# Where the sums of the second product live: accumulators in SBUF, or copies added by DMAs into DRAM

## The chip, the cores and the metric

One core of a Trainium2 chip runs the kernel. The metric is the time of one execution in device microseconds; less is better. The matrix products run on TensorE (PE in the profile, its weight loads PEld), the elementwise work on VectorE (DVE) and ScalarE (ACT), some on GpSimd (POOL); SyncE (SP) issues most transfers. Each engine has one queue and takes its instructions in order. Products accumulate in PSUM, in banks of 512 f32 per partition.

## The reference

```python
def reference(q, k, v, shift_k, ssm_k, ssm_D, w1, w2):   # S=2048, D=576, Dff=4608
    x  = q
    xn = layernorm(x)
    # H3: a short causal convolution of k, times v, then a long one over S by FFT
    k_shift = sum(k_pad[:, t:t + S] * shift_k[:, ks - 1 - t] for t in range(4))
    kv = k_shift * v
    y  = irfft(rfft(pad(kv)) * rfft(pad(ssm_k)))[:S] + kv * ssm_D
    a  = xn * y
    # feed-forward
    b  = relu(xn @ w1) @ w2
    return x + a + b
```

The sum `x + a + b` has a row for each of the 2048 positions and 576 columns. All of it is f32; the kernel splits each f32 operand of a product into a high and a low part (names `hi`, `lo`, `hh`, `ll`) and multiplies three of the four pairs.

## The kernel before, in words

**Two jobs share the core.** The feed-forward part (FFN) is a fixed sequence of "visits"; the long convolution is a generator, `conv`, whose steps are issued in between.

**The FFN.** The 4608 hidden columns are cut into `NPAIR` = 18 weight pairs of 256 columns, the 2048 rows into `NB` = 4 blocks b of 512. A half of the run treats two blocks (`HB` = 2): for each pair n it visits both blocks s, so there are 72 visits. In a visit, `quad` (L538) makes the first product in four stages, with seven products by sums of operands in place of eight, and two PSUM banks `psb` and `psa`. ScalarE copies one product to `m5`; VectorE adds it to the banks (the pair's sums, L574 and L577); `relu` (L528) writes `hh` on ScalarE (L531) and `ll` on VectorE (L532). The second product is cut into `unit`s (L589): one 128-row tile t (i in a block), one half h of the columns (`NH` = 288), 6 or 12 matmuls into a bank `pso`, of which there are three. `phase` puts eight units of a block into a list, and `fill` takes some after each stage of a quad.

**The sums.** Behind its matmuls a unit adds its bank on VectorE into an accumulator in SBUF, which was loaded with x: for block 0 with the layernorm's factor `rstd` (L610, `scalar_tensor_tensor`), else plainly (L614). A unit's bank is free for the next but two when that add is done. The accumulators of the first half go to DRAM (`fin`) when complete, and the last stage of the convolution adds them to its rows and stores these; those of the second half get the convolution's rows added (L935) and are stored by the last units, the very last row tile by SP and ScalarE's queue (L618).

**The convolution.** A Fourier transform by matmuls with constant matrices, in stages: z (nothing of it yet), loading `kt`; k (transform of `ssm_k`: `stack` splits a tile `ks` on ScalarE L649 and VectorE L650, `first` multiplies and copies the bank on ScalarE, L657); x (the short convolution on VectorE, rows `c` and `e`, L742 to L751, then `xs` split and multiplied in the same way); m (the products of the spectra and the inverse step); o (the last transform; rows `y`, gated with the normalized x at L927 by VectorE, added up at L935). Constants come by POOL's DMAs, into three buffers.

**Who sets the order.** `tick(cost)` is called after each stage of a quad and every six matmuls of a unit. It counts the FFN's work and lets `conv` take one step when it has fallen behind its share; a step's price is one of `W_FK`, `W_FX`, `W_FM`, `W_FO`. Inside a step, `here()` holds elementwise instructions back in their queue until the places of `done["acc"]` and `done["act"]`, the last sum on VectorE and the last marked activation on ScalarE, so that they stand right behind these. Before, `done["acc"]` is set by the units' adds alone.

**The weights.** SP loads them (`r`), ScalarE rounds them to the high part (L453, L511), POOL subtracts for the low part (L424) and makes the sums of weights (L478).

Of the kernel before, what the change touches and what calls it, by code (L numbers as in the profile page):

```python
# [49 lines left out]
SHARE = 0.96  # L50
# [3 lines left out]
W_FK, W_FX, W_FM, W_FO = 1.73, 3.5, 1.94, 2.2  # L54
# [6 lines left out]
SUMS = {"b11": 0, "t1": 1, "t2": 2, "t3": 3, "t4": 4}  # L61
# [44 lines left out]
def h3_ffn_kernel(ctx: ExitStack, tc, x, k, v, shift_k, ssm_k, ssm_D, w1, w2, fwd, inv, mid, out):  # L106
# [23 lines left out]
    fin = dram.tile([HT // 2, P, 2, D], F32, name="fin")  # L130
# [23 lines left out]
    def load_x(t, tag, bufs, **queues):  # L154
        pair = xp.tile([P, 2, D], F32, tag=tag, name=f"acc{t}", bufs=bufs)
        move(pair, x, slice(t, t + 2), **queues)
        return pair

    def load_acc(t, **queues):
        pairs[t] = load_x(t, f"acc{t // BT % HB}", BT // 2, **queues)  # L160
        acc[t], acc[t + 1] = pairs[t][:, 0, :], pairs[t][:, 1, :]
# [120 lines left out]
    def first_xT(srcs):  # L282
# [5 lines left out]
        neg = zp.tile([P, BT], F32, tag="neg", name="neg")  # L288
        behind = None
        for t in range(BT):  # L290
            if t % 2 == 0:
                pair = row_tiles(t)
            xn = pair[:, t % 2, :]
            if t % 2 == 0:
                with tc.issue_after(behind.ins) if behind else nullcontext():
                    stats(t, srcs[t])
                    behind = centred(xn, srcs[t], t)
            else:
                nc.scalar.activation(xn, srcs[t], AF.Copy, scale=-1.0 / D,
                                     accum_out=neg[:, t:t + 1])  # L300
                done["act"] = nc.scalar.activation(xn, srcs[t], AF.Identity,
                                                   bias=neg[:, t:t + 1])
# [11 lines left out]
        with tc.issue_after(done["dve"].ins):  # L314
            for t in range(1, BT, 2):
                stats(t, srcs[t])
            inv_std(0, BT)

    def second_xT(srcs):
# [7 lines left out]
        xn = []  # L327
        for t in range(BT, HT):
            if t % 2 == 0:
                pair = row_tiles(t)  # L330
            xn.append(pair[:, t % 2, :])
            normalized(xn[-1], srcs[t], t)
# [229 lines left out]
    def quad(n, s, m):  # L562
# [11 lines left out]
        nc.vector.tensor_tensor(pa[:, other], pb[:, first], m5, OP.add)  # L574
        yield
        run_seq(pb[:, first], product(n, s, "s3", "t3"))
        nc.vector.tensor_tensor(pb[:, other], pb[:, first], m5, OP.add)  # L577
# [9 lines left out]
    work = []  # L587

    def unit(ns, s, b, i, h, last):  # L589
# [15 lines left out]
        for i, (a, m) in enumerate(seq):  # L605
            nc.tensor.matmul(ps[:, :NH], a, m, start=i == 0, stop=i == len(seq) - 1)  # L606
            if i % 6 == 5:
                tick(6 * NH)
        if b == 0:
            done["acc"] = nc.vector.scalar_tensor_tensor(  # L610
                acc[t][:, dc], ps[:, :NH], rstd[:, t:t + 1], acc[t][:, dc],
                op0=OP.mult, op1=OP.add)
        else:
            done["acc"] = nc.vector.tensor_tensor(acc[t][:, dc], ps[:, :NH], acc[t][:, dc],  # L614
                                                  OP.add)
        if final and t == T - 1:
            for u, queue in ((0, nc.sync), (1, nc.scalar)):
                queue.dma_start(out[u, :, t, dc], acc[t][halves(u)[0], dc])  # L618
        elif last and h:
            if t < HT:  # L620
                if t % 2:
                    nc.sync.dma_start(fin[t // 2], pairs[t - 1])
            elif t == T - 2:
                move(acc[t], out, t, store=True)
            elif t % 2:
                move(pairs[t - 1], out, slice(t - 1, t + 1), store=True)
# [38 lines left out]

    def conv():
# [3 lines left out]

        with tc.tile_pool(name="fk", bufs=2) as fp:
# [18 lines left out]
            def prepare(t, h):  # L690
                stk = fp.tile([P, NH], F32R, tag="stk", name=f"ks{t}_{h}", bufs=3)
# [22 lines left out]

# [440 lines left out]
```

## Time and profile before

| | |
|---|---|
| time, median of 3 runs | 1132.33 us (1128.83 to 1133.09) |
| the profiled execution, its time | 1130.09 us |
| the profiled execution, its span | 1128.1 us, mean granted clock 0.98 |
| instructions in the span | 21092 |
| bytes moved by DMA | 166.75 MB, mean 148 GB/s |
| span, stage z / k / gap / x | 0 to 204 / 204 to 309 / 309 to 343 / 343 to 547 us |
| span, gap / m / gap / o / tail | to 571 / to 953 / to 974 / to 1110 / to 1128.1 us |

A row of a view by stretches gives, per engine, the busy time and in parentheses the number of instructions, then the granted clock as a share of full speed, the mean busy share of 16 DMA engines (it can go over 1 where packets overlap) and GB/s. A row of groups gives line, engine, operation, out<-in by the program's names, shape and type, count, then busy time in us, mean ns of one, and the engine's idle time just before them with what ended it. A row of the waits gives who waited for whom: us in total, times, longest. A row of the timeline gives start, length, and in brackets the idle time ahead. The stages' bounds were taken from the first and last instruction of each.

### The profile page before, as it was taken

The page shows a single profiled execution, that of the slowest core. Times are in us where ns is not written, and L with a number is a line of the kernel's source. Part 1 is how long each engine was busy: PE and PEld are TensorE (multiplying, and loading weights), DVE is VectorE, ACT ScalarE, POOL GpSimd, SP SyncE. Part 2 cuts the span into 40 slices and gives each one's busy share as a digit, 9 for nine tenths or more (in the row PEclk, how much of TensorE's full clock was granted, in tenths as well). Part 3 has the DMA queues.
Part 4 walks back from the last instruction along what each step waited for, and adds up shares of the span by engine and source line. Part 5 has one row for each costly group of instructions (what it writes and reads, how often), then busy time and mean ns, then how long its engine had stood idle before and what let it go on. Part 6 is the DMA issues. An engine that isn't in the chain of part 4 may idle for free.

```text
span 1128.1 us, 21092 instructions
## 1 busy us (share of the span) xinstructions
PE 1067.1 (95%) x7761; PEld 1025.5 (91%) x7761; DVE 803.6 (71%) x1309; ACT 668.3 (59%) x1454; POOL 489.6 (43%) x492
## 2 busy tenths in 40 slices
PE   8979998999988798898999999999999999999998
PEld 5779998999988788898998999999999999999897
DVE  5578733677759999888466667676576665589985
ACT  4434422798824444443368878888887887465451
POOL 3243444455435444564433344433343443545541
PEclk9998998999998999998999999999999999999999
DMA  6035598355574554453894434442334432666654
GB/s 173 25 96 189 214 147 133 114 161 165 167 200 143 159 149 136 140 166 106 300 321 129 128 108 119 121 135 87 111 113 133 119 116 93 168 176 175 206 167 105
DMA packets 139154, 166.75 MB, mean 148 GB/s; under 512 B 47566, under 2 KB 99536, under 8 KB 138541
## 3 DMA queue, kind: packets, MB, share of 16 engines
q1 hardware_dynamic: 126156, 151.24, 46.7%
q0 software_dynamic: 12576, 13.44, 5.2%
q8 instruction: 61, 1.00, 0.4%
q10 hardware_dynamic: 320, 0.74, 0.3%
q14 instruction: 41, 0.33, 0.1%
HBM read 122.12 MB, written 43.25 MB: 147 GB/s over the span
## 4 chain that ended last, share of the span: by engine, by line
PE 67%; DVE 17%; DMA 5%; SPq 4%; issue 3%; ACT 3%; POOL 1%; POOLq 0%; DVEq 0%; ACTq 0%
PE pso L606 28%; PE psb L525 18%; PE psa L525 8%; PE psf L824 6%; DVE e L745 3%; SPq L679 3%; PE psh L525 2%; DVE c L746 2%; PE psf L656 2%; DMA r<-in_w 1%; DVE xs L650 1%; DVE ll L532 1%; DVE acc L614 1%; DVE acc L610 1%; DVE c L751 1%
## 5 line engine op out<-in xcount | busy, mean ns | idle before, releaser
L606 PE MATMUL pso<-w,hh 128*128 128x288 f32 x2304 | 469.9, 298 | 11.0 <-DVE acc L610 6.9
L606 PEld LDWEIGHTS pso<-w,hh 128*128 128x128 f32 x2304 | 371.6, 190 | 20.9 <-DVE acc L610 7.8
L424 POOL TENSOR_TENSOR g<-r,g 128x512 fp32r<-128x512 f32 (+2 forms) x178 | 207.4, 1174 | 379.2 <-ACT g L453 297.4
L606 PE MATMUL pso<-w,ll 128*128 128x288 f32 x1152 | 320.8, 297 | 3.9 <-DVE ll L532 3.9
L525 PE MATMUL psb<-t,g 128*128 128x256 f32 x1632 | 248.2, 287 | 26.2 <-DVE psa L574 14.1
L525 PEld LDWEIGHTS psb<-t,g 128*128 128x128 f32 x1632 | 220.3, 191 | 33.7 <-DVE psa L574 16.7
L606 PEld LDWEIGHTS pso<-w,ll 128*128 128x128 f32 x1152 | 211.3, 190 | 6.5 <-DVE ll L532 4.8
L424 POOL TENSOR_TENSOR w<-r,w 128x576 fp32r<-128x576 f32 x72 | 114.6, 1593 | 73.1 <-ACT w L511 72.9
L478 POOL TENSOR_TENSOR r<-r 128x256 f32<-128x256 f32 x136 | 115.6, 868 | 62.2 <-DMA r<-in_w 59.8
L614 DVE TENSOR_TENSOR acc<-pso,acc 128x288 f32<-128x288 f32 x224 | 96.7, 450 | 57.7 <-PE pso L606 56.9
L525 PE MATMUL psa<-b,g 128*128 128x256 f32 x816 | 122.1, 286 | 0.0
L531 ACT ACTIVATE hh<-psa 128x512 fp32r<-128x512 f32 x68 | 40.7, 598 | 127.2 <-PE psa L525 126.8
L525 PEld LDWEIGHTS psa<-b,g 128*128 128x128 f32 x816 | 109.8, 193 | 0.2
L453 ACT ACTIVATE g<-r 128x512 fp32r<-128x512 f32 (+2 forms) x178 | 91.2, 535 | 29.3 <-POOL r L478 12.1
L532 DVE SCALAR_TENSOR_TENSOR ll<-psa,hh 128x512 fp32r<-128x512 f32 x68 | 46.7, 686 | 39.7 <-ACT hh L531 39.5
L531 ACT ACTIVATE hh<-psb 128x512 fp32r<-128x512 f32 x68 | 40.7, 598 | 49.3 <-PE psb L525 46.5
L532 DVE SCALAR_TENSOR_TENSOR ll<-psb,hh 128x512 fp32r<-128x512 f32 x68 | 46.6, 686 | 29.1 <-ACT hh L531 28.7
L650 DVE TENSOR_TENSOR ks<-kt,ks 64x288 fp32r<-64x288 f32 x64 | 54.4, 849 | 17.3 <-ACT ks L649 15.7
L525 PE MATMUL psb<-b,g 128*128 128x256 f32 x408 | 62.1, 286 | 0.0
L860 DVE TENSOR_TENSOR k<-psf,k 128x288 f32<-128x288 f32 x64 | 28.8, 454 | 46.0 <-ACT sw L859 37.9
L525 PEld LDWEIGHTS psb<-b,g 128*128 128x128 f32 x408 | 55.1, 193 | 0.0
L610 DVE SCALAR_TENSOR_TENSOR acc<-pso,rstd,acc 128x288 f32<-128x288 f32 x80 | 39.4, 511 | 19.7 <-PE pso L606 19.1
(138 smaller groups left out, 1778.7 us busy)
## 6 DMA issues: line engine op xcount, KB each, us to landing
r<-in_w SPq DMA_DIRECT2D x72, 288.0 KB, 4.0
r<-in_w SPq DMA_DIRECT2D x35, 512.0 KB, 4.1
zk<-zk SPq DMA_DIRECT2D x32, 288.0 KB, 2.7
zx<-zx SPq DMA_DIRECT2D x32, 288.0 KB, 3.5
ztk<-zk SPq DMA_DIRECT2D x32, 288.0 KB, 3.1
ztx<-zx SPq DMA_DIRECT2D x32, 288.0 KB, 2.9
zy<-vo SPq DMA_DIRECT2D x32, 288.0 KB, 3.4
zo<-zy SPq DMA_DIRECT2D x32, 288.0 KB, 3.6
```

Source lines behind the costliest of these rows:

```text
L424: return nc.gpsimd.tensor_tensor(dst, src, hi, OP.subtract)
L453: nc.scalar.activation(hi, src, AF.Copy)
L478: nc.gpsimd.tensor_tensor(dst, a, b, op)
L525: nc.tensor.matmul(ps, a, m, start=start and i == 0, stop=i == len(seq) - 1, skip_group_check=not start)
L531: done["act"] = nc.scalar.activation(hh, ps, AF.Relu)
L532: lows.append(nc.vector.scalar_tensor_tensor(ll, ps, 0.0, hh, op0=OP.max, op1=OP.subtract))
L606: nc.tensor.matmul(ps[:, :NH], a, m, start=i == 0, stop=i == len(seq) - 1)
L610: done["acc"] = nc.vector.scalar_tensor_tensor(acc[t][:, dc], ps[:, :NH], rstd[:, t:t + 1], acc[t][:, dc], op0=OP.mult, op1=OP.add)
L614: done["acc"] = nc.vector.tensor_tensor(acc[t][:, dc], ps[:, :NH], acc[t][:, dc], OP.add)
L650: nc.vector.tensor_tensor(dst[other], src[own], dst[own], OP.subtract)
L679: nc.sync.dma_start(kt[halves(h)[0], d:d + KD, :], src)
L824: nc.tensor.matmul(ps[:, :NH], a, m[:, cols], start=n == 0, stop=n == 2)
```

## The change

- A DRAM buffer `total`, [4, 128, 4, 576], takes the place of `fin` and of all accumulators in SBUF. Eight transfers from DRAM to DRAM put x into it at the start.
- A unit copies its bank into one half of a tile `g` in SBUF: ScalarE (L630, L635) in stages z, x and o, VectorE (L632, L637) in k and m. For block 0 the copy multiplies with `rstd`. Each second unit has POOL issue a transfer that adds the tile (288 KB) into `total`. `g` has four buffers.
- The second half's last units load their part of `total` back (`load_total`, into tiles of the same ring), add the bank on VectorE and store the halves; both blocks now go row tile by row tile. The convolution's rows y for the second half are added into `total` by POOL's transfers.
- `done["acc"]` is set by the pair's sums as well, so the convolution's VectorE work can stand right behind them.
- `tick` takes steps once per unit (behind its first six matmuls) and up to two at a stage of a quad; the steps' prices change.
- In o, the gate's normalization goes to ScalarE (an activation with `rstd` and `shift`), VectorE multiplies. Some buffers become more (`stk`, `k`, `zt`); the first rows of x are normalized in place.

The diff, its core:

```diff
-SHARE = 0.96
+SHARE = 0.965
-W_FK, W_FX, W_FM, W_FO = 1.73, 3.5, 1.94, 2.2
+W_FK, W_FX, W_FM, W_FO = 1.875, 3.98, 2.02, 2.03
+BY_ACT = "zxo"
+G_BUFS = 4
...
-    fin = dram.tile([HT // 2, P, 2, D], F32, name="fin")
+    total = dram.tile([NB, P, BT, D], F32, name="total")
...
+    def load_total(t, h):
+        b, i = divmod(t, BT)
+        pair = xp.tile([P, 2, NH], F32, tag="g", name=f"last{t}_{h}", bufs=G_BUFS)
+        nc.sync.dma_start(pair, total[b, :, i:i + 2, h * NH:(h + 1) * NH])
+        for n in range(2):
+            acc[t + n, h] = pair[:, n]
...
     def quad(n, s, m):
-        nc.vector.tensor_tensor(pa[:, other], pb[:, first], m5, OP.add)
+        done["acc"] = nc.vector.tensor_tensor(pa[:, other], pb[:, first], m5, OP.add)
...
-        nc.vector.tensor_tensor(pb[:, other], pb[:, first], m5, OP.add)
+        done["acc"] = nc.vector.tensor_tensor(pb[:, other], pb[:, first], m5, OP.add)
...
     def unit(ns, s, b, i, h, last):
-        for i, (a, m) in enumerate(seq):
-            nc.tensor.matmul(ps[:, :NH], a, m, start=i == 0, stop=i == len(seq) - 1)
-            if i % 6 == 5:
-                tick(6 * NH)
+        for c, (a, m) in enumerate(seq):
+            nc.tensor.matmul(ps[:, :NH], a, m, start=c == 0, stop=c == len(seq) - 1)
+            if c % 6 == 5:
+                tick(6 * NH, c == 5)
+        if final:
+            if h == 0 and i % 2 == 0:
+                for m in range(2):
+                    load_total(t, m)
+            to = acc[t, h]
+            done["acc"] = nc.vector.tensor_tensor(to, ps[:, :NH], to, OP.add)
+            for u, queue in ((0, nc.sync), (1, nc.scalar if t == T - 1 else nc.sync)):
+                queue.dma_start(out[u, :, t, dc], to[halves(u)[0]])
+            return
+        if i % 2 == 0:
+            g = xp.tile([P, 2, NH], F32, tag="g", name=f"sum{ns[0]}_{t}_{h}", bufs=G_BUFS)
+            parts_[0] = g
+        to, src = parts_[0][:, i % 2], ps[:, :NH]
+        act = stage[0] in BY_ACT
         if b == 0:
-            done["acc"] = nc.vector.scalar_tensor_tensor(
-                acc[t][:, dc], ps[:, :NH], rstd[:, t:t + 1], acc[t][:, dc],
-                op0=OP.mult, op1=OP.add)
+            if act:
+                done["act"] = nc.scalar.activation(to, src, AF.Copy, scale=rstd[:, t:t + 1])
+            else:
+                done["acc"] = nc.vector.tensor_scalar(to, src, rstd[:, t:t + 1], None,
+                                                      op0=OP.mult)
+        elif act:
+            done["act"] = nc.scalar.activation(to, src, AF.Copy)
         else:
-            done["acc"] = nc.vector.tensor_tensor(acc[t][:, dc], ps[:, :NH], acc[t][:, dc],
-                                                  OP.add)
...
+            done["acc"] = nc.vector.tensor_copy(to, src)
+        if i % 2:
+            nc.gpsimd.dma_start(total[b, :, i - 1:i + 1, dc], parts_[0], accum_op=OP.add)
...
     def phase(ns, s, b, last):
-        if last and b == NB - 1:
+        if last and b >= HB:
...
              def gate(i):
-                        nc.vector.scalar_tensor_tensor(ys[i], rest[i][1], mv[:, t, 0:1], ys[i],
-                                                       op0=OP.subtract, op1=OP.mult)
+                        q = rest[i][1]
+                        nc.scalar.activation(q, q, AF.Identity, scale=rstd[:, t:t + 1],
+                                             bias=shift[:, t:t + 1])
+                        nc.vector.tensor_tensor(ys[i], ys[i], q, OP.mult)
...
              def add(i):
+                        nc.gpsimd.dma_start(total[t // BT, :, t % BT, :], ys[i],
+                                            accum_op=OP.add)
...
-    def tick(cost):
+    def tick(cost, steps=1):
+        was = clock["ffn"]
+        clock["ffn"] += cost
+        if clock["done"] or was < clock["until"]:
             return
         clock["conv"] += rate[0] * cost
+        for _ in range(steps):
+            if clock["conv"] < 0:
+                return
...
          load_w2(1, h)
+    for b in range(NB):
+        for u in range(U):
+            nc.sync.dma_start(total[b, halves(u)[0]], x[u, :, b * BT:(b + 1) * BT, :])
...
-                tick(W_STAGE[st])
+                tick(W_STAGE[st], 2)
```

What this moves is seen best in the queues. A row is a line, an operation, out<-in with serial numbers, and a shape. First VectorE in stage x, in the visit of pair 12 and its first block, from the pair's second sum (L577, in the changed kernel L581) on. Before:

```order
L577 TENSOR_TENSOR psb12_1_4566<-psb12_1_4566,m5_12_1_4580 128x256
L745 TENSOR_TENSOR e6_3_4606<-k3_4046,sk_3443 128x576
L746 TENSOR_TENSOR c6_4525<-c6_4525,e6_3_4606 128x576
L610 SCALAR_TENSOR_TENSOR acc0_95<-pso11_1_1_4833,rstd_84,acc0_95 128x288
L532 SCALAR_TENSOR_TENSOR ll12_1_0_4679<-psa12_1_4567,hh12_1_0_4678 128x512
L751 TENSOR_TENSOR c6_4525<-c6_4525,v6_4466 128x576
L745 TENSOR_TENSOR e7_1_4715<-k6_4463,sk_3443 128x576
L610 SCALAR_TENSOR_TENSOR acc2_98<-pso11_2_1_4876,rstd_84,acc2_98 128x288
L746 TENSOR_TENSOR c7_4699<-c7_4699,e7_1_4715 128x576
L650 TENSOR_TENSOR xs6_0_4659<-c6_4525,xs6_0_4659 64x576
```

Now, on VectorE at the same place:

```order
L581 TENSOR_TENSOR psb12_1_4670<-psb12_1_4670,m5_12_1_4684 128x256
L760 TENSOR_TENSOR c7_4834<-k7_4746,sk_3514 128x576
L763 TENSOR_TENSOR e7_1_4851<-k6_4564,sk_3514 128x576
L536 SCALAR_TENSOR_TENSOR ll12_1_0_4782<-psa12_1_4671,hh12_1_0_4781 128x512
L764 TENSOR_TENSOR c7_4834<-c7_4834,e7_1_4851 128x576
L663 TENSOR_TENSOR xs6_0_4788<-c6_4642,xs6_0_4788 64x576
L663 TENSOR_TENSOR xs6_1_4802<-c6_4642,xs6_1_4802 64x576
L763 TENSOR_TENSOR e7_2_4891<-k5_4406,sk_3514 128x576
L536 SCALAR_TENSOR_TENSOR ll12_1_1_4822<-psb12_1_4670,hh12_1_1_4821 128x512
L764 TENSOR_TENSOR c7_4834<-c7_4834,e7_2_4891 128x576
L578 TENSOR_TENSOR psa13_1_4863<-psb13_1_4862,m5_13_1_4876 128x256
```

The units' adds (`acc<-pso`) are gone from the queue, and a visit holds ten rows of the convolution between its four rows of the pair. Second, SP at the end of the program. Before, its last rows:

```order
L898 DMA zo31_13886<-zy_87 128x576
L910 DMA ft7_13741<-fin_88 128x576
L150 DMA out_0<-acc8_6989 64x1152 x2
L150 DMA out_0<-acc10_6992 64x1152 x2
L150 DMA out_0<-acc12_6740 64x1152 x2
```

Now, SP's last rows (`last` are the tiles loaded back from `total`; x2 and x4 count transfers in a row):

```order
L621 DMA out_0<-last10_1_14403 64x288 x2
L167 DMA last12_1_14465<-total_88 128x2x288
L621 DMA out_0<-last10_1_14403 64x288 x2
L621 DMA out_0<-last10_0_14401 64x288 x2
L621 DMA out_0<-last10_1_14403 64x288 x2
L621 DMA out_0<-last12_0_14463 64x288 x2
L621 DMA out_0<-last12_1_14465 64x288 x2
L621 DMA out_0<-last12_0_14463 64x288 x2
L621 DMA out_0<-last12_1_14465 64x288 x2
L167 DMA last14_0_14507<-total_88 128x2x288
L167 DMA last14_1_14509<-total_88 128x2x288
L621 DMA out_0<-last14_0_14507 64x288 x2
```

The last tiles' loads from `total` stand behind the stores of the tiles before them. Third, SP near the start. Before:

```order
L150 DMA acc4_226<-in_x 64x1152 x2
L150 DMA acc6_229<-in_x 64x1152 x2
L435 DMA r1_1_232<-in_w1 128x4x256
L437 DMA r1_1_232<-in_w1 64x256 x2
L444 DMA r2_1_0_239<-in_w2 128x2x288
```

Now, on SP:

```order
L151 DMA acc4_228<-in_x 64x1152 x2
L151 DMA acc6_231<-in_x 64x1152 x2
L1068 DMA total_88<-in_x 64x2304 x8
L439 DMA r1_1_234<-in_w1 128x4x256
L441 DMA r1_1_234<-in_w1 64x256 x2
```

The eight transfers into `total` now stand ahead of the second pair's w1 (`r1_1`). ScalarE splits that w1 a little later in its queue, now ahead of the second block's first copies (`b1_1`):

```order
L182 ACTIVATE q4_314<-q4_314 128x4
L630 ACTIVATE sum0_2_1_461<-pso0_2_1_454,rstd_84 128x288
L630 ACTIVATE sum0_2_1_461<-pso0_3_1_463,rstd_84 128x288
L457 ACTIVATE g1_0_472<-r1_1_234 128x512
L226 ACTIVATE b1_1_296<-psf_325 128x512
```

In the kernel before, those copies (`b1_1`, L218) follow the row of `q4` at once, and the split of the second pair stands behind them.

More of the change, by code (lines that the diff above doesn't have):

```diff
@@ L326, in second_xT @@
             inv_std(BT, BT)
[L327 to L332, printed above, removed]
+        xn = [srcs[t] for t in range(BT, HT)]
+        for i, row in enumerate(xn):
+            normalized(row, row, BT + i)
         for c in range(5):
@@ L664, in here @@
             yield
+    stage = ["z"]
+    shift = const.tile([P, T], F32, name="shift")
     def conv():
+        stage[0] = "k"
         with tc.tile_pool(name="fk", bufs=2) as fp:
@@ L932, in add @@
                     t = order[i]
-                    to, more = (ys[i], rest[i][2]) if t < HT else (acc[t], acc[t])
-                    with here():
-                        nc.vector.scalar_tensor_tensor(to, ys[i], rstd[:, t:t + 1], more,
-                                                       op0=OP.mult, op1=OP.add)
                     if t < HT:
-                        move(to, out, t, store=True, queues=(nc.gpsimd, nc.gpsimd))
-                    else:
+                        with here():
+                            nc.vector.tensor_tensor(ys[i], ys[i], rest[i][2], OP.add)
+                        move(ys[i], out, t, store=True, queues=(nc.gpsimd, nc.gpsimd))
+                    else:
+                        nc.gpsimd.dma_start(total[t // BT, :, t % BT, :], ys[i],
+                                            accum_op=OP.add)
                         added.add(t)
-            for n in range(2):
+            for n in range(3):
                 load_z(n)
@@ L1120, in h3_ffn_kernel @@
             phase([n], s, b, True)
-        if half == 1 and m == 0:
-            base = HT + (1 - second) * BT
-            for t in range(base, base + BT, 2):
-                load_acc(t)
     while work:
```

78 lines of the change are left out of this document (33 added, 45 removed).

## The prediction

> **What bounds the kernel now.** I read the busy times first, then the span cut at the stages of the convolution, then the chain, the waits and one engine's groups in the stage that loses most.
>
> ```profile
> PE 1067.1 (95%) x7761; PEld 1025.5 (91%) x7761; DVE 803.6 (71%) x1309; ACT 668.3 (59%) x1454; POOL 489.6 (43%) x492
> ```
>
> TensorE is busy for 95% of the span, so the whole span can only shrink by what PE loses somewhere. The next view cuts the span into z (before the convolution's first step), k, the gap behind it, x, a gap, m, a gap, o and the tail. Columns: stretch, length, then busy time and count of PE, PEld, DVE, ACT and POOL, the granted clock, the DMA share, GB/s.
>
> ```profile
> 0.00:204.00 204.00, 184.33 (x1209) 166.54 (x1210) 119.22 (x240) 75.57 (x155) 77.69 (x83) 0.96 0.61 135
> 204.00:309.00 105.00, 103.05 (x777) 100.27 (x777) 81.62 (x121) 92.24 (x178) 56.09 (x68) 1.00 0.54 163
> 309.00:343.00 34.00, 29.94 (x217) 29.28 (x216) 20.39 (x34) 8.87 (x19) 13.29 (x15) 0.95 0.63 170
> 343.00:547.00 204.00, 181.16 (x1279) 171.87 (x1278) 182.31 (x245) 87.03 (x187) 101.84 (x97) 0.96 0.50 146
> 547.00:571.00 24.00, 24.00 (x185) 23.64 (x185) 8.86 (x17) 8.01 (x17) 11.52 (x12) 1.00 1.04 401
> 571.00:953.00 382.00, 379.64 (x2869) 373.32 (x2869) 257.59 (x427) 315.00 (x725) 152.25 (x136) 1.00 0.42 125
> 953.00:974.00 21.00, 21.00 (x164) 20.82 (x164) 7.64 (x15) 6.86 (x15) 10.49 (x12) 1.00 0.77 205
> 974.00:1110.00 136.00, 131.24 (x984) 127.45 (x983) 117.91 (x199) 73.52 (x160) 65.37 (x71) 1.00 0.56 163
> 1110.00:1128.10 18.10, 12.75 (x95) 12.34 (x93) 8.11 (x16) 1.19 (x2) 1.04 (x2) 0.91 0.58 147
> ```
>
> Stage m is the clean one: 382.0 / 2869 = 0.1331 us per matmul. At that rate x needs 1279 x 0.1331 = 170.2 us and takes 204.0, a loss of 33.8. The gap ahead of x loses 34.0 - 28.9 = 5.1, o 136.0 - 131.0 = 5.0, k 105.0 - 103.4 = 1.6. x is also the one stage where VectorE is nearly full: 182.31 of 204, 89%. The chain through x, the groups on VectorE (busy time, mean ns, idle before) and the waits say what that does:
>
> ```profile
> by line: DVE e L745 14.4%; PE psb L525 12.8%; PE pso L606 12.8%; DVE c L746 9.9%; issue 8.3%; DVE xs L650 6.7%; PE psa L525 5.7%; DVE c L751 4.7%; DVE c L742 4.0%; DVE ll L532 3.3%; DVE acc L614 3.1%; PE psf L656 3.0%; DMA r<-in_w 2.3%; DVE
> ```
> ```profile
> L745 DVE TENSOR_TENSOR e<-k,sk 128x576 f32<-128x576 f32 x42 | 42.6, 1014 | 0.5
> L746 DVE TENSOR_TENSOR c<-c,e 128x576 f32<-128x576 f32 x48 | 42.1, 878 | 0.4
> L650 DVE TENSOR_TENSOR xs<-c,xs 64x576 fp32r<-64x576 f32 x32 | 31.5, 983 | 1.2 <-ACT xs L649 0.2
> L610 DVE SCALAR_TENSOR_TENSOR acc<-pso,rstd,acc 128x288 f32<-128x288 f32 x32 | 15.7, 510 | 5.4 <-PE pso L606 5.1
> L614 DVE TENSOR_TENSOR acc<-pso,acc 128x288 f32<-128x288 f32 x24 | 10.5, 449 | 1.9 <-PE pso L606 1.9
> L532 DVE SCALAR_TENSOR_TENSOR ll<-psa,hh 128x512 fp32r<-128x512 f32 x13 | 8.9, 685 | 3.7 <-ACT hh L531 3.7
> L574 DVE TENSOR_TENSOR psa<-psb,m 128x256 f32<-128x256 f32 x14 | 5.9, 421 | 2.2 <-PE psb L525 2.2
> ```
> ```profile
> L745 DVE TENSOR_TENSOR e<-k,sk x42: 743/759/1979, 336.4 to 532.1; 128x576 f32<-128x576 f32 x42
> ```
> ```profile
> PEld psb L525 <- DVE psa L574: 14.0, 6, 4.7
> PE psb L525 <- DVE psa L574: 12.6, 6, 4.5
> ACT xs L649 <- DVE c L751: 12.1, 5, 3.6
> ```
>
> The convolution's long elementwise rows fill VectorE, some at 1979 ns against a minimum of 743. The pair's sum L574 stands in the same queue, and six times PE waits up to 4.5 us for it. That wait is what a lighter VectorE can shorten.
>
> **The change, part by part.**
>
> *Sums leave VectorE in x.* The 56 sums of the second product shown above (15.7 + 10.5 = 26.2 us) go to ScalarE as copies. The new order also spreads the stage over more matmuls (1271 rows of PE's order between its first and last convolution matmul before, 1444 now), so it lasts 1444 x 0.1331 = 192.2 us without stalls; these 173 rows bring about 1.6 visits of two L574-like and two L532-like rows, 1.6 x 2 x (0.42 + 0.69) = 3.5 us. VectorE then holds 182.3 - 26.2 + 3.5 = 159.6 of 192.2 us, 83%. In o, at 117.91 of 136, 87%, PE lost only 3.7% of its time, so below that a stage hardly stalls on load alone; what is left is the queue's order, and the convolution's steps now stand right behind the pair's sums instead of ahead of them. Of 33.8 us I leave 4 as stall: **-30**, between -20 (one 1 us row of the convolution still ahead of a sum in about 14 visits) and -36 (the gap ahead of x gains too). ScalarE's 59 copies there cost 59 x 0.41 (the copy zk below) = 24 us beside 87.03, 111 of 192 us: covered unless its queue order bites (first rival).
>
> *Stage o.* 37 sums and 8 adds leave VectorE, 32 copies and 15 gate activations go to ScalarE:
>
> ```profile
> L614 DVE TENSOR_TENSOR acc<-pso,acc 128x288 f32<-128x288 f32 x37 | 16.0, 448 | 7.5 <-PE pso L606 7.2
> L935 DVE SCALAR_TENSOR_TENSOR acc<-y,rstd,acc 128x576 f32<-128x576 f32 x8 | 8.5, 1067 | 0.1
> ```
>
> VectorE drops by 24.5 us to 93 of 136 (or of 125: the stage is denser, 901 rows for 978), and ScalarE rises by 32 x 0.41 + 15 x 0.74 (an estimate, from ks below) = 24.2 to 98. Of the 5.0 us lost I take **-4**, between -5 and +3.
>
> *Stage k* is denser: 704 rows of PE for 776, and its ScalarE was the fullest engine.
>
> ```profile
> L649 ACT ACTIVATE ks<-kt 64x288 fp32r<-64x288 f32 x63 | 46.4, 736 | 1.3
> L657 ACT ACTIVATE zk<-psf 128x288 f32<-128x288 f32 x63 | 25.3, 402 | 8.9 <-DMA zk<-zk 3.4 <-PE psf L656 2.4 <-ACT g L453 1.3
> ```
>
> The stage's own 71.7 us stay, the other 20.5 of 92.24 shrink with the rows to 18.6: 90.3 of 704 x 0.1331 = 93.7 us, 96%. VectorE holds 89% in x and loses; here I take **+3** (0 to +8). Sums on VectorE are copies of the same size as L614, 0.45 us, so z, k and m keep their load: 0 (-2 to +2), m being covered by VectorE's 257.59 of 382.
>
> *The 144 accumulating DMAs (288 KB each) and 8 for y, all issued by POOL.* No such transfer is in the trace.
>
> ```profile
> q1 hardware_dynamic: 126156, 151.24, 46.7%
> zy<-vo SPq DMA_DIRECT2D x32, 288.0 KB, 3.4
> kt<-in_ssm_k SPq DMA_DIRECT2D x16, 288.0 KB, 7.3
> ```
> ```profile
> L643 POOL DMA_DIRECT2D wx<-in_fwd x29 | 16.0, 551 | 35.8 <-PE psf L656 35.8
> ```
>
> Issuing: 0.55 us (L643) to 0.9 us, I take 0.65: 152 x 0.65 = 99 us of POOL's 638 idle us; each waits in POOL's queue for its two copies, ahead of the weights' low halves, which stand visits ahead of their use. Transfer: by q1, 46.7% of 1128.1 us for 151.24 MB is 3.48 us of all engines per MB, 1.03 us per 288 KB. An accumulate is at least that; its destination is also read, so I take 2.06, and as end the slowest transfer of that size in the trace (kt, 7.3 against 3.4 us to land): 2.2. In x 29 of them add 60 us to 102 busy of 204 (share 0.50): 162 of 192, hidden, and the four buffers cover 26 us of landing at one per 6.6 us. In o 15 and 8 for y add 47 us to 76 of 136: hidden, just. Cost 0, up to +3.
>
> *Start.* Eight DRAM-to-DRAM copies (4.72 MB) go onto SP ahead of the second pair's w1.
>
> ```profile
> 6.16 6.27 SPq L150 DMA_DIRECT2D acc<-in_x  x4
> 17.73 0.37 SPq L435 DMA_DIRECT2D r<-in_w  x1
> 33.28 1.09 ACT L218 ACTIVATE b<-psf 128x512 fp32r<-128x512 f32 x2 [4.46 <-PE psf L343]
> 42.88 1.55 ACT L453 ACTIVATE g<-r 128x512 fp32r<-128x512 f32 x4
> ```
>
> Eight issues at 6.27 / 4 = 1.57 us push that load from 17.73 to 12.4 + 12.5 = 25 us, and 4.72 MB at the 401 GB/s of the gap behind x take 11.8 us: it lands near 37 to 40. The row of 42.88 shows the slack, but ScalarE's split of it now stands ahead of the copies that began at 33.28. **+4** (0 to +12, at half that rate).
>
> *The load of kt.* Seven accumulates fall where the DMA engines are already full and a weight sum waits:
>
> ```profile
> 183.32 2.08 POOL L478 TENSOR_TENSOR r<-r 128x256 f32<-128x256 f32 x3 [8.31 <-DMA r<-in_w]
> 187.33 1.65 PE L525 MATMUL psb<-t,g 128*128 128x256 f32 x6 [4.58 <-DVE ll L532]
> 82.44 0.97 PE L525 MATMUL psb<-t,g 128*128 128x256 f32 x6 [2.98 <-DVE psb L577]
> ```
>
> 7 x 1.03 to 7 x 2.06 is 7 to 14 us more in the queues; part meets slack: **+3** (0 to +10). After 4.58 us idle the six matmuls took 1.65 us, after 2.98 us 0.97: a long stall costs more than itself. The Trainium skill ("TensorE: Matmul & The Clock Gate", Part 1: The HAM clock gate) has the array at half rate after an idle window of about 3.4 us, until about 3.4 us of work. The trace agrees in these two rows; by that rule a stall in the start that exceeds the window would cost some 1.7 us on top, an estimate.
>
> *The tail.* The last sums now come from DRAM.
>
> ```profile
> 1122.46 0.29 PE L606 MATMUL pso<-w,ll 128*128 128x288 f32 x1
> 1123.26 1.44 SPq L618 DMA_DIRECT2D out<-acc  x2
> ```
> ```profile
> ft<-fin SPq DMA_DIRECT2D x8, 288.0 KB, 3.8
> ```
>
> Today the end is 5.4 us behind the last matmul. The load of last14 stands on SP behind stores that wait for the adds of last12: two to four stores of 0.72 us, its issue and 3.8 us of landing, while PE's last four units (3.2 us) can't all run ahead, with three banks. **+5** (0 to +9).
>
> Sum: 1130.1 - 30 - 4 + 3 + 4 + 3 + 5 = **1111 us**, from the profiled execution (span 1128.1; 2.2 us under the median of the runs, inside their 4.3 us spread).
>
> **The rivals.**
>
> *Banks behind ScalarE.* A copy of a sum stands in ScalarE's queue behind xs, which waits up to 3.6 us for VectorE's c; three banks of 1.6 us hold 3.2 to 4.8. For it: 5 such waits, 12.1 us. Against: c comes sooner. If each of 16 row blocks gives 0.7 us, x gains 11 less: **1122**.
>
> *A late front.* Start and kt both at their ends, +22 for +7: **1126**. For it the 24 to 28 us before the new load lands; against it the slack to 42.88.
>
> *Accumulates fill the DMA engines, slower.* In x 102 us are free, 90 after the stage's shortening: 90 / 29 = 3.1 us each; in o 60 / 23 = 2.6. That is the point where it decides, 2.5 to 3 plain transfers. At four (4.12 us) x gets 29 x 4.12 - 90 = +29 and o 23 x 4.12 - 60 = +35, PE waiting for banks, these for copies, these for buffers: **1175**. Nothing in the trace shows such a price, nor excludes it. The Trainium skill ("DMA: Bandwidth & Descriptors", Anatomy of one DMA — SWDGE (gpsimd) path) gives about 2.0 us and bytes over 436e3 for a transfer issued there, 2.7 us for this size, an estimate; by that this rival never happens, and no run here shows it for an accumulate.
>
> *The change does not act:* x loses its time to the long rows themselves, whatever else VectorE has. Then x gives back 11, as much as the other terms take: **1130**.
>
> **How the numbers follow.** Forecast 0.57 (own range 1098 to 1124), banks 0.15, late front 0.11, accumulates 0.12, no action 0.05. A change under 0.5% (5.7 us on 1132.3) can't be told from none: faster means below 1126.6. Faster: 0.56 + 0.13 + 0.05 = 0.74; same: 0.01 + 0.02 + 0.05 + 0.03 = 0.11; slower: 0.12 + 0.01 + 0.02 = 0.15. Leaving out the accumulates' rival and the best 0.07, the range is 1095 to 1137.
>
> **What would show it.** Right: in x VectorE under 85%, PE's waits for psa's sum under 6 us, the granted clock 1.00, each matmul near 0.135 us. The start: the second pair's w1 landing before 40 us. The tail: last matmul to end about 10 us. Wrong: accumulates taking over 10 us to land or POOL issues over 1.2 us, a DMA share over 0.95 in x or o, ScalarE's queue named in PE's waits for banks, or k over 100 us.

## The result, and the profile after

The changed kernel takes 1175.51 us (median of 4 runs, 1171.58 to 1177.72) against 1131.56 us for the kernel before: ratio 1.0387, interval 1.0353 to 1.0422, slower. The forecast was 1111, faster; the time lies outside the range, and beside the 1175 that one rival gave. That nearness is chance, as shown below: its price was not met.

The busy times and the queue of POOL's transfers, from the page of the changed kernel:

```profile
PE 1075.1 (92%) x7761; PEld 1026.9 (88%) x7761; DVE 776.7 (66%) x1169; ACT 728.7 (62%) x1605; POOL 655.9 (56%) x644
q0 software_dynamic: 52896, 58.28, 32.5%
```

VectorE did get lighter (803.6 to 776.7 us) and ScalarE fuller, as the change says. POOL went from 489.6 to 655.9 us, and its queue of transfers from 5.2% to 32.5% of the DMA engines. The same cut by stages (z, k, gap, x, gap, m, gap, o, tail; columns as before):

```profile
0.00:216.00 216.00, 184.91 (x1206) 167.02 (x1207) 105.42 (x214) 85.33 (x182) 104.12 (x106) 0.94 0.83 182
216.00:321.50 105.50, 95.96 (x708) 92.00 (x708) 80.02 (x110) 91.42 (x179) 66.85 (x76) 1.00 0.77 193
321.50:357.00 35.50, 27.15 (x190) 26.25 (x188) 15.21 (x24) 10.71 (x24) 17.28 (x18) 0.86 0.85 205
357.00:581.50 224.50, 200.25 (x1445) 190.28 (x1446) 190.45 (x205) 113.69 (x258) 141.79 (x135) 0.98 0.75 182
581.50:612.00 30.50, 30.50 (x235) 30.10 (x234) 11.88 (x24) 8.46 (x20) 14.90 (x14) 1.00 1.08 307
612.00:994.00 382.00, 375.34 (x2809) 364.72 (x2808) 253.90 (x413) 314.07 (x720) 210.15 (x190) 1.00 0.67 150
994.00:1016.00 22.00, 22.00 (x170) 21.66 (x169) 7.46 (x12) 10.42 (x25) 13.04 (x16) 1.00 0.78 190
1016.00:1147.00 131.00, 122.90 (x902) 119.57 (x901) 102.96 (x153) 91.88 (x199) 86.11 (x90) 0.97 0.98 240
1147.00:1173.40 26.40, 16.10 (x112) 15.34 (x110) 9.39 (x20) 2.74 (x5) 1.70 (x4) 0.87 0.57 146
```

Length less 0.1331 us per matmul is what PE loses in a stage. For x that is 224.5 - 1445 x 0.1331 = 32.2 us. By stage, us lost:

| | z | k | gap | x | m | o | tail |
|---|---|---|---|---|---|---|---|
| before | 43.1 | 1.6 | 5.1 | 33.8 | 0 | 5.0 | 5.5 |
| after | 55.5 | 11.3 | 10.2 | 32.2 | 8.1 | 10.9 | 11.5 |
| difference | +12.4 | +9.7 | +5.1 | -1.6 | +8.1 | +5.9 | +6.0 |

Two things have to be explained: why x gave back 1.6 us instead of 30, and why every other stage lost. VectorE's rows in x and POOL's groups show the first:

```profile
L764 DVE TENSOR_TENSOR c<-c,e 128x576 f32<-128x576 f32 x44 | 50.5, 1148 | 0.7
L763 DVE TENSOR_TENSOR e<-k,sk 128x576 f32<-128x576 f32 x41 | 47.9, 1168 | 0.4
```
```profile
L639 POOL DMA_DIRECT2D total<-sum x144 | 184.1, 1284 | 74.1 <-DVE sum L637 22.0 <-ACT sum L635 15.0 <-ACT sum L630 12.1
L428 POOL TENSOR_TENSOR g<-r,g 128x512 fp32r<-128x512 f32 (+2 forms) x178 | 222.3, 1300 | 206.5 <-ACT g L457 175.0 <-PE pso L611 25.3 <-PE psf L669 3.2
L656 POOL DMA_DIRECT2D wx<-in_fwd x32 | 24.0, 751 | 23.8 <-PE psf L669 22.4 <-PE psa L529 1.0 <-issue 0.3
```

The sums that left VectorE, in x's own bounds (343 to 547 us of the kernel before), are 49 and took 22.8 us:

```profile
L610 DVE SCALAR_TENSOR_TENSOR acc<-pso,rstd,acc 128x288 f32<-128x288 f32 x25 | 12.3, 509 | 4.4 <-PE pso L606 4.2
L614 DVE TENSOR_TENSOR acc<-pso,acc 128x288 f32<-128x288 f32 x24 | 10.5, 449 | 1.9 <-PE pso L606 1.9
```

The prediction's 56 sums, 26.2 us, are of 326 to 547 us, 17 us more than x; so are its rows e and c. In x alone e averaged 1021 ns before and now 1168, c 871 and now 1148: the convolution's rows that stayed got longer. An accumulating transfer takes POOL 1284 ns to issue, twice my 0.65 us. The longest e, on the timeline of the changed kernel, VectorE first and then POOL:

```profile
486.66 4.82 DVE L763 TENSOR_TENSOR e<-k,sk 128x576 f32<-128x576 f32 x1
```
```profile
485.65 1.30 POOL L428 TENSOR_TENSOR g<-r,g 128x512 fp32r<-128x512 f32 x1
486.90 1.42 POOL L428 TENSOR_TENSOR w<-r,w 128x576 fp32r<-128x576 f32 x1
488.27 1.26 POOL L639 DMA_DIRECT2D total<-sum  x1
489.07 1.79 POOL L428 TENSOR_TENSOR g<-r,g 128x512 fp32r<-128x512 f32 x1
490.31 1.73 POOL L639 DMA_DIRECT2D total<-sum  x1
```

A row that takes 742 ns alone takes 4822 while POOL works without a pause through weights and issues. Over all 147 rows of x on VectorE with two operands in SBUF, by what of POOL they overlap (worked out from the trace's records):

| overlapped on POOL | rows | mean ns | longest |
|---|---|---|---|
| nothing | 53 | 749 | 759 |
| issues alone | 18 | 754 | 760 |
| tensor work alone | 38 | 1029 | 1933 |
| both | 38 | 1971 | 4822 |

A long row meets more of POOL just by being long, so the last mean says less than the first two lines: without POOL's tensor work no row took over 760 ns. Before, the 146 such rows of x averaged 985 ns, now 1138: 147 x 0.153 = 22.5 us come back of the 22.8 that the sums took away. The rows that read PSUM (the pair's sum L578, `ll` from psa) did not stretch, 431 and 678 ns in x against 420 and 685 before, but they stand in the queue behind the ones that do. The Trainium skill ("SBUF — State Buffer", SBUF: two separate sides) has VectorE and GpSimd take a shared pair of ports as an exclusive lock, for two operands in SBUF too. The table agrees in which rows stretch. A row that waited once for the longest tensor row of POOL that this e overlaps, 1.79 us, would take 2.5 us with its own 0.74; this e took 4.82. That such a lock is the cause is read from the overlap and not tested by itself.

The wait that the change was to shorten did go, and others took its place. Four of PE's waits for VectorE in x, of the changed kernel (us in total, times, longest):

```profile
PE psb L529 <- DVE psb L581: 9.4, 5, 3.5
PE psb L529 <- DVE ll L536: 6.7, 9, 1.3
PE psf L669 <- DVE xs L663: 5.3, 6, 2.2
PE psb L529 <- DVE psa L578: 0.7, 1, 0.7
```

Before, these four were 1.3, 0.8, 2.0 and 12.6 us.

The second, the loss everywhere else, shows best in z, where `kt` is loaded:

```profile
199.72 2.09 POOL L482 TENSOR_TENSOR r<-r 128x256 f32<-128x256 f32 x3 [14.42 <-DMA r<-in_w]
201.15 0.80 PE L529 MATMUL psb<-t,g 128*128 128x256 f32 x2 [12.68 <-ACT g L457]
```

POOL waits 14.42 us for a weight's load (8.31 before), and PE idles for 12.68 us (4.58 before).

### The profile page after: what moved, and what is told of

Its sections match the earlier page's. It is cut to its first block, busy times and chain, and to the rows that moved or that the text cites. A ratio compares the mean times of both kernels' runs of the same rounds, so it can differ in the third digit from the quotient of the medians.

```text
span 1173.4 us, 21588 instructions
## 1 busy us (share of the span) xinstructions
PE 1075.1 (92%) x7761; PEld 1026.9 (88%) x7761; DVE 776.7 (66%) x1169; ACT 728.7 (62%) x1605; POOL 655.9 (56%) x644
## 3 DMA queue, kind: packets, MB, share of 16 engines
q0 software_dynamic: 52896, 58.28, 32.5%
## 5 line engine op out<-in xcount | busy, mean ns | idle before, releaser
L428 POOL TENSOR_TENSOR g<-r,g 128x512 fp32r<-128x512 f32 (+2 forms) x178 | 222.3, 1300 | 206.5 <-ACT g L457 175.0
L529 PE MATMUL psb<-t,g 128*128 128x256 f32 x1632 | 248.2, 287 | 45.0 <-ACT g L457 12.7
L639 POOL DMA_DIRECT2D total<-sum x144 | 184.1, 1284 | 74.1 <-DVE sum L637 22.0
L482 POOL TENSOR_TENSOR r<-r 128x256 f32<-128x256 f32 x136 | 126.4, 959 | 110.7 <-DMA r<-in_w 109.1
L578 DVE TENSOR_TENSOR psa<-psb,m 128x256 f32<-128x256 f32 x68 | 29.0, 427 | 70.3 <-PE psb L529 54.1
L663 DVE TENSOR_TENSOR ks<-kt,ks 64x288 fp32r<-64x288 f32 x64 | 58.2, 909 | 19.2 <-ACT ks L662 17.7
L637 DVE COPY sum<-pso 128x288 f32<-128x288 f32 x123 | 52.9, 449 | 26.8 <-PE pso L611 26.6
L535 ACT ACTIVATE hh<-psb 128x512 fp32r<-128x512 f32 x68 | 40.5, 596 | 23.3 <-PE psb L529 22.5
```

The costliest lines, as they stand in the source:

```text
L428: return nc.gpsimd.tensor_tensor(dst, src, hi, OP.subtract)
L482: nc.gpsimd.tensor_tensor(dst, a, b, op)
L529: nc.tensor.matmul(ps, a, m, start=start and i == 0, stop=i == len(seq) - 1, skip_group_check=not start)
L535: done["act"] = nc.scalar.activation(hh, ps, AF.Relu)
L578: done["acc"] = nc.vector.tensor_tensor(pa[:, other], pb[:, first], m5, OP.add)
L637: done["acc"] = nc.vector.tensor_copy(to, src)
```

## The experiments

Theories: A, POOL's queue: issuing costs by its time there. B, the DMA engines: the added bytes come in the way of the loads. C, the order or the copies cost. Ratios are to the kernel before, with their interval.

### Order alone, and transfers left out or moved

`e1_order` puts the order into the kernel before:

```diff
-SHARE, W_FK, W_FX, W_FM, W_FO = 0.96, 1.73, 3.5, 1.94, 2.2
+SHARE, W_FK, W_FX, W_FM, W_FO = 0.965, 1.875, 3.98, 2.02, 2.03
+        done["acc"] = nc.vector.tensor_tensor(pa[:, other], pb[:, first], m5, OP.add)
...
+                tick(6 * NH, c == 5)
...
+                tick(W_STAGE[st], 2)
```

> The kernel before with the changed order alone: the pair's sums set the place of the convolution's VectorE work, one step per unit and up to two per stage of a quad, the changed prices and share; sums stay on VectorE in SBUF, no larger buffers. If the order is what costs (theory C), x stays above 220 us or another stage loses, and the time is 1140 to 1165. If the order is harmless and the loss comes with the copies and the accumulating transfers (A or B), 1115 to 1135.

1113.78 us, 0.9852 (0.9828 to 0.9877): a little under the range for A or B. C falls for the order, which by itself gains 1.5%. The loss in x is 21.7 us.

`e2_noacc` leaves out the changed kernel's line `nc.gpsimd.dma_start(total..., parts_[0], accum_op=OP.add)`, so the sums are copied and never added.

> The changed kernel without the 144 accumulating transfers of the sums (the second product is left out of the result but for the last units); copies, order and the 8 transfers for y stay. Theories A (POOL's issues hold VectorE's rows) and B (the DMA engines are too full, so weights come late) both say 1110 to 1125, with x near 197 us and PE's 12.7 us wait at 201 us gone. Theory C (order or copies cost) says 1145 or more.

1109.73 us, 0.9809 (0.9773 to 0.9846). The span is 1105.4 us, 22.7 under before; my sum had 19 for the whole change. C falls for the copies too. The 66 us between this and 1175.5 belong to the 144 transfers. The rows of x with two operands in SBUF average 1058 ns here, 73 more than before, though POOL issues none of the transfers and is busy for 115.10 of 212 us in x (101.84 of 204 before): about half of the stretch of 153 ns came without them.

`e3_plain` and `e4_sp` keep the transfers but store plainly, so the sums are overwritten and not added:

```diff
-            nc.gpsimd.dma_start(total[b, :, i - 1:i + 1, dc], parts_[0], accum_op=OP.add)
+            nc.gpsimd.dma_start(total[b, :, i - 1:i + 1, dc], parts_[0])      # e3_plain
+            nc.sync.dma_start(total[b, :, i - 1:i + 1, dc], parts_[0])        # e4_sp
```

> The changed kernel with plain stores in place of the accumulating transfers, still issued by POOL at the same places (the sums are overwritten, not added). A: POOL's queue does the same as before, VectorE's longest row in x stays over 3 us, and x stays near 220: 1145 to 1170. B: the DMA engines get back 144 x 1 us, x falls under 205, 1115 to 1130.

> As the last one, but the plain stores are issued by SP instead of POOL (sums overwritten). A: POOL's queue is free of them, VectorE's longest row in x falls to about 2 us and x under 200: 1110 to 1125. B: the same transfer time as with POOL issuing, so the same time as the last run within 6 us. C: 1145 or more.

1132.48 us, 1.0013 (0.9993 to 1.0032), and 1117.21 us, 0.9874 (0.9849 to 0.9899). Over e2, moving the same bytes costs 7.5 us by SP and 22.8 by POOL: A holds for 15.3 us, B for the other 43 between e3 and the change, or so it seemed; e3 itself lies between what A and B had it at. POOL's issue in e3 is also shorter, and the DMA queue lighter:

```profile
L639 POOL DMA_DIRECT2D total<-sum x144 | 106.7, 741 | 82.8 <-DVE sum L637 26.7 <-ACT sum L635 14.0 <-ACT sum L630 13.8
q0 software_dynamic: 25248, 58.28, 17.0%
```

POOL's other transfers are the queue's line in e2:

```profile
q0 software_dynamic: 13728, 15.80, 6.8%
```

That is 0.068 x 1105.4 = 75.2 us. A plain store of 288 KB takes (0.170 x 1127.7 - 75.2) / 144 = 0.81 us of the 16 engines, an accumulating one (0.325 x 1173.4 - 75.2) / 144 = 2.13.

### Doubling one cost at a time

`e5_sp2` has SP store each tile twice, `e6_pool2` has POOL store it in two halves, both plainly:

```diff
+            for to_ in (total, twice):                                        # e5_sp2
+                nc.sync.dma_start(to_[b, :, i - 1:i + 1, dc], parts_[0])
...
+            for m in range(2):                                                # e6_pool2
+                nc.gpsimd.dma_start(total[b, :, i - 1 + m:i + m, dc], parts_[0][:, m:m + 1])
```

> Plain stores of each pair of copies by SP as before, but two of them (one into total, one into a second DRAM buffer), so the DMA engines get about 2 x 1 us per pair, as much as one accumulate took (2.1 us), and POOL stays free. If the time on the DMA engines is what an accumulate costs beyond a plain store (B), the run loses most of those 43 us: 1145 to 1165. If it is POOL's longer issue (A: 1.28 us for an accumulate, 0.74 for a plain store), 1115 to 1125.

> Plain stores issued by POOL, each pair of copies as two transfers of half the size: POOL spends about 1.2 us per pair, as on an accumulate, the DMA engines move no more bytes than with one plain store. A (POOL's issue time holds its queue and VectorE): 1150 to 1175. B (time on the DMA engines): 1130 to 1140, near the 1132 us of the single plain store.

1116.58 us, 0.9883 (0.9842 to 0.9925): twice the stores in SP's queue cost nothing over e4 that the intervals show. The queue lines of e4 and e5 give (0.688 x 1113.4 - 0.583 x 1112.2) / 144 = 0.82 us of the engines for each further store:

```profile
q1 hardware_dynamic: 168524, 196.08, 58.3%
```
```profile
q1 hardware_dynamic: 207692, 238.55, 68.8%
```

The queues q1 and q0 together fill 75.5% of the engines' span in e5 (68.8 and 6.7) and 76.5% in the change (44.0 and 32.5). So fuller DMA engines alone are not what costs. And e6 took 1142.16 us, 1.0103 (1.0071 to 1.0134): 288 issues of 566 ns cost 10 us over 144 of 741. That lies between both expectations; its order of steps also shifted (1308 rows of PE in x for 1446), so only the total is read.

`e7_late` issues each accumulating transfer one pair of units later, with five buffers.

> The changed kernel with each accumulating transfer issued one pair of units later, and five buffers, so that POOL no longer waits for the copies (74 us of idle time ahead of those issues). If POOL's waits are what bunches its queue, 1150 to 1160; if issue time or DMA time costs, 1170 to 1180.

1182.73 us, 1.0459 (1.0421 to 1.0496). This is above both expectations. POOL's idle time ahead of these issues stayed, 82.1 us for 74.1, so the edit didn't take the waits away, and whether they matter is open.

`e8_done` changes in the kernel before only the two lines that set `done["acc"]` at the pair's sums.

> The kernel before with one thing of the order alone: the pair's sums set the place of the convolution's VectorE work, old steps and prices. If that placement is what made the order's run faster (1113.8 against 1130.5 us), 1112 to 1120; if the steps and prices did it, 1126 to 1134.

1116.55 us, 0.9867 (0.9835 to 0.9899): the placement makes most of the order's gain, 13.7 of 16.7 us. With the stage cut at its first and last convolution matmul, x loses 21.5 us for 34.0.

### Fewer pieces, and the transfers by themselves

`e9_rows` has the changed kernel add a whole row tile at a time, 128 pieces of 2304 bytes in place of 256 of 1152 (a piece is one run without a gap in DRAM); its units go row tile by row tile for that:

```diff
+        if ns[0] >= 1 or (last and b >= HB):
             order = [(i, h) for i in range(BT) for h in range(2)]
...
+            nc.gpsimd.dma_start(total[b, :, i, :].rearrange("p (h d) -> p h d", h=2), parts_[0],
+                                accum_op=OP.add)
```

> The changed kernel with the units in order of row tiles, so that an accumulating transfer takes one whole row tile, 128 rows of 2304 bytes in place of 256 of 1152: the same bytes and the same number of transfers, half the pieces. If the number of pieces sets what POOL spends on an issue (1.28 us) and that is what costs (A), the issue falls to about 0.8 us and the time to 1140 to 1160. If it is the adding itself on the DMA engines (B), 1165 to 1180.

1158.11 us, 1.0222 (1.0180 to 1.0265), 17 less than the change. The rows' bytes and number are those of the change, but for 8 early transfers of the old form:

```profile
L641 POOL DMA_DIRECT2D total<-sum x136: 842/874/1935, 97.9 to 1117.7; - x136
L644 POOL DMA_DIRECT2D total<-sum x8: 1174/1208/1671, 26.1 to 81.6; - x8
```

The middle one of the three times is the median, in ns. So 128 pieces take POOL 0.87 us to issue and 256 take 1.21. The 17 us are not all POOL's: by the queue's share, (0.308 x 1155.9 - 75.2) / 144, a transfer also takes 1.95 us of the 16 engines in place of 2.13.

The next three add transfers to e1's kernel, from the accumulators in SBUF into an unused buffer: accumulating, plain, and accumulating 16 columns of 288.

```diff
+        if i % 2 and not final:
+            nc.gpsimd.dma_start(total[b, :, i - 1:i + 1, dc], pairs[t - 1][:, :, dc],
+                                accum_op=OP.add)
```

> The order's run (1113.8 us: old sums on VectorE in SBUF, new order) with 144 accumulating transfers added at the places of the changed kernel, each adding the accumulator's part to an unused DRAM buffer. No copies and no other change. If the accumulating transfers by themselves are what the changed kernel lost by (A or B), 1160 to 1185; if it needs the copies on ScalarE and VectorE too, under 1140.

> As the last one with plain stores by POOL in place of the accumulating ones: A and B both say what POOL's plain stores cost in the changed kernel, 15 to 23 us over 1113.8: 1128 to 1138.

> As the run with accumulating transfers in the order's kernel, but of 16 columns in place of 288: as many transfers and pieces, 16 KB each in place of 288. A (POOL's time to issue them): the same time as with 288 columns within 8 us. B (the adding of the bytes on the DMA engines): 1125 to 1140, near the plain stores.

1188.16, 1144.13 and 1154.64 us; 1.0483 (1.0433 to 1.0532), 1.0104 (1.0064 to 1.0144) and 1.0192 (1.0159 to 1.0225). Over e1's 1113.8 that is +74, +30 and +41. Accumulating transfers cost by themselves, copies or not, and 16 KB each cost more than half of what 288 KB do. Neither A nor B alone fits e12. The plain store cost more than I expected.

`e13_thin` makes the same cut in the changed kernel, so most of each sum is left out:

```diff
+            nc.gpsimd.dma_start(total[b, :, i - 1:i + 1, h * NH:h * NH + 16],
+                                parts_[0][:, :, :16], accum_op=OP.add)
```

> The changed kernel with its accumulating transfers cut to 16 of 288 columns (the rest of the sums is left out): as many transfers and pieces, copies, order and POOL's queue unchanged. Beside the plain stores (1132.5) and the full accumulation (1175.5) it splits the 43 us between them: POOL's time to issue (A) if 1150 or more, adding the bytes on the DMA engines (B) if under 1140. By the old sums' runs (1154.6 thin, 1144.1 plain, 1188.2 full) I expect both, 1143 to 1155, with the stretch before 216 us back near 45 us of loss and x's loss still near 30.

1143.55 us, 1.0099 (1.0068 to 1.0130). POOL's issues are those of the change, the queue's share is not:

```profile
L639 POOL DMA_DIRECT2D total<-sum x144 | 183.8, 1279 | 75.6 <-DVE sum L637 24.3 <-ACT sum L635 15.0 <-DVE sum L632 13.0
q0 software_dynamic: 52896, 18.17, 14.4%
```

This splits the 65.8 us: 33.8 stay without most of the bytes (1109.7 to 1143.6), which I put down to POOL's queue, and 32.0 come with the bytes (to 1175.5). The first part isn't POOL's queue alone: a transfer of 16 KB still takes (0.144 x 1141.3 - 75.2) / 144 = 0.62 us of the 16 engines, but 0.82 us more of them from SP's queue cost nothing (e5). By stage, us lost, from the profiles of the three (stages cut at their first and last convolution matmul, so the change's figures differ by up to 0.4 from the table above):

| | z | k | gap | x | m | o | tail |
|---|---|---|---|---|---|---|---|
| e2, no transfers | 36.4 | 9.7 | 1.7 | 14.7 | -0.2 | -0.6 | 11.3 |
| e13, POOL's queue | 43.0 | 6.0 | 8.0 | 29.7 | 5.3 | 5.5 | 11.5 |
| the change, and bytes | 55.6 | 11.4 | 10.6 | 32.2 | 8.3 | 11.1 | 11.8 |

In x it is POOL's queue, 15.0 of 17.5 us; the bytes take most in z, 12.6 us, where `kt` is loaded. In e2 the order shifted, and x holds 1482 rows of PE for the 1446 of the other two; but e5, with 1446 and its sums stored by SP, loses 12.1 us in x. VectorE's e in x, of e13 and then of e4, where POOL is free of the issues:

```profile
L764 DVE TENSOR_TENSOR e<-k,sk 128x576 f32<-128x576 f32 x41 | 48.4, 1179 | 0.4
```
```profile
L763 DVE TENSOR_TENSOR e<-k,sk 128x576 f32<-128x576 f32 x42 | 45.1, 1075 | 0.4
```

Over all rows with two operands in SBUF, e4's 150 average 1046 ns and e13's 146 average 1142: 146 x 0.096 = 14 us, near the 17.0 us by which e13 loses more in x (29.7 and 12.7). More than half of what POOL's queue costs falls outside x, and there it isn't traced to a wait.

### A better version

`e14_wider_x` and `e15_wider_x2` are e1 with other prices of steps:

```diff
+W_FK, W_FX, W_FM, W_FO = 1.78, 4.4, 1.93, 2.03      # e14_wider_x
+W_FK, W_FX, W_FM, W_FO = 1.73, 4.8, 1.9, 2.0        # e15_wider_x2
```

> The order's kernel (1113.8 us) with other prices of the steps: the x stage is spread over 1474 of PE's rows in place of 1363, the m stage is 100 rows denser. If VectorE's load in x still holds PE there (21.7 us of loss), 1103 to 1111; if only the single rows ahead of a pair's sum do, no change.

> As the last one, x spread over 1562 rows: 1098 to 1108 if VectorE's load holds PE in x and ScalarE still has room in the denser m stage (82% busy before); above the last one if m begins to lose.

1110.70 us, 0.9807 (0.9772 to 0.9842), and 1110.13 us, 0.9804 (0.9776 to 0.9832). e14 just makes its range, e15 misses its own. x loses 13.9 and 16.4 us for 21.7, m begins to lose 2. Against e1's 1113.8 the intervals overlap, and against each other; with e15's 1110.13, 2.0% under before, they are the fastest complete kernels here. Both keep the sums in SBUF and send nothing more.

## Why the prediction was wrong

The step that failed is the term for the accumulating DMAs, "Cost 0, up to +3": they cost 65.8 us (1109.7 without them, 1175.5 with them), 33.8 that stay with 16 KB each and 32.0 for the rest of the bytes. Both halves of its reason failed: that their issues fit into POOL's idle time, and that their transfers are hidden. Without them the change comes 20.8 us under before, near the 19 of my sum. That nearness is luck in part: x gave less than its term, k lost more, and z gained where I had a loss.

- **"152 x 0.65 = 99 us of POOL's 638 idle us"**: the 144 alone took 184.1 us. I priced the issue by wx at 0.55 us, a transfer of 128 KB; the accumulating ones take 1.21 us at 256 pieces and 0.87 at 128. That idle time was also the pauses in which VectorE's rows ran unhindered. "Cost 0" came to 33.8 us here.
- **The accumulates' time on the DMA engines, 2.06 us**: 2.13, right. "Hidden" was wrong, 32.0 us. A share of 0.75 in x is not full, and x shows 2.5 us of it; z, k and o lost 23.6, with 0.98 in o.
- **The sums leave VectorE in x, -30**: -1.6 measured. Without the transfers it is -19.1 (33.8 to 14.7), of which the placement alone makes -12. A second step failed here: I took 159.6 us for VectorE in x as what was left after subtracting rows, at their old durations, and 3.4 us too many of them (26.2 for 22.8). It held 190.45 us of 224.5. The 3.4 and the stretch of 22.5 bring 159.6 to 185.5; the rest isn't accounted for. Without the transfers (e2) VectorE still held 180.78 of 212, with 148 x 0.073 = 10.8 us of stretch. The trace of before had such rows, the e of 1979 ns that I quoted; I did not ask which engine overlapped them. The wait that I named, for psa's sum, did shrink (12.6 to 0.7 us), but waits for psb's sum, `ll` and xs came in its place.
- **The rival that ended at 1175**: its sign was right and its time by chance. It put 4.12 us on a transfer, in x and o, and needed over 2.6; the price was 2.13, and half of the loss came from POOL's queue, which it didn't hold. Read it as not met. From issue to landing an accumulating transfer took 6.0 us in the median, not the 2.7 of the estimate beside this rival; a plain store from the same queue took 4.3 (e3).
- **Start and kt, +7**: z lost 12.4 more. Without the transfers it gained 6.7, so the start was priced too dear, and the accumulates in z too cheap.
- **k, +3**: +9.7; +8.1 without the transfers (there with 670 rows of PE). That is the upper end of what I gave, but not shown to be ScalarE's 96%: PE's waits in k of the changed kernel name the load of `wk` for 2.9 us and ScalarE for 3.0.
- **o, -4**: +5.9; -5.6 without the transfers, near the forecast. **m, 0**: +8.1, and nothing without them.
- **The tail, +5**: +6.0, right and for the reason given. From the timeline of the changed kernel:

```profile
1163.20 1.07 SPq L167 DMA_DIRECT2D last<-total  x2
1166.49 1.34 DVE L619 TENSOR_TENSOR last<-pso,last 128x288 f32<-128x288 f32 x3 [7.11 <-DMA last<-total]
1167.01 0.85 PE L611 MATMUL pso<-w,hh 128*128 128x288 f32 x2 [5.72 <-DVE last L619]
```

PE's last unit waits 5.72 us for the add that waits for the last loads.
- **Banks behind ScalarE**: no wait of PE for a bank that ScalarE holds is among the long ones. **A late front**: PE waited 5.19 us at 39 us for ScalarE's copies, 2.25 us in e2; the wait of 12.68 us while kt is loaded is longer.
- **The signs**: VectorE under 85% in x (84.8%) and the short wait for psa's sum came as for a right forecast; issues on POOL over 1.2 us (1.28), o's share of 0.98 and k's 105.5 us came as for a wrong one. The first two don't see that the stage itself became longer.

What stays open is why added bytes cost 32 us from POOL's queue, while 144 further plain stores, 0.82 us of the engines each, cost nothing from SP's (e5), and why half of the stretch in x came without the transfers. Accumulating can't be told from the queue here, since no accumulating transfer ran from SP.

## What to carry to other kernels

Work taken off a full engine is worth its time only if the rows that stay keep theirs: look in the trace for rows far over their shortest, find which engine overlaps them, and ask what the change gives that engine. POOL's idle time is not free room when VectorE works on two operands in SBUF, and an issue on POOL takes longer with more pieces, and longer again when it accumulates. Try the order of the work by itself before moving data: two lines that set a place in the queue gained 1.3% here, and the data's new place lost 5.5% against the order alone (1113.8 to 1175.5).

## What the runs showed of the hardware

- POOL's issue grows with pieces and not with bytes, and is longer for accumulating. In medians, plain stores took 0.56 us for 128 pieces (144 KB, e6) and 0.73 us for 256 (288 KB, e11); accumulating ones of 288 KB took 0.87 us for 128 pieces and 1.21 us for 256 (e9), and 1.20 us for 256 pieces with 16 KB in all (e12):

```profile
L618 POOL DMA_DIRECT2D total<-acc x144: 1172/1197/1705, 27.5 to 1114.7; - x144
```

- An accumulating transfer took 2.13 us of the 16 engines for 288 KB into DRAM, 2.6 times a plain store's 0.81 from the same queue (e3).
- A row of VectorE with two operands in SBUF did not always get its turn between two instructions of POOL: the e of 4822 ns spans the ends of three tensor rows of POOL. Beside POOL's DMA issues alone, no such row in x took over 760 ns.
